# A long convolution beside a linear attention block: reciprocal by ln and exp on ACT, four more matmuls of zeros, and a new order of units

## The chip, the cores and the metric

One core of a Trainium2 chip runs the kernel. The metric is the device time of one execution in microseconds (us). The engines are named as in the profile: PE (TensorE matmul), PEld (its weight loads), DVE (VectorE), ACT (ScalarE), POOL (GpSimd), SP (SyncE, which issues all DMAs here). The engines work in parallel, each through its own queue in order; PSUM is the memory that PE writes.

## The reference

Two independent blocks over a sequence of S = 2048 rows and D = 576 columns, in bf16, whose outputs are set side by side.

```python
# A: gated long convolution
k_shift = sum over t<4 of k[s-t] * shift_k[:, t]
kv = k_shift * v
y  = causal convolution of kv with ssm_k (length 2048) along s, by FFT of length 4096
out_A = q * (y + kv * ssm_D)
# B: linear attention, 32 heads of 18
q, k, v = x @ wqkv
phi(t) = where(t > 0, t + 1, exp(t)) + 1e-6
kv = phi(k)^T v ; z = sum_s phi(k)         (per head)
o  = (phi(q) kv) / (phi(q) . z + 1e-6)
out_B = o @ wo
```

## The kernel before, in words

The program is a list of some 300 units, written out by hand as the string ORDER. A loop at the end of the kernel takes them one after the other, and each emits its instructions on the engines' queues. So the position in ORDER alone sets the order on every engine: a unit further ahead stands further ahead in each queue that it touches. What follows the slash (`k.8/3`) names the buffers: PSUM is cut into four pairs of banks, 0 to 3, and a unit that takes a pair waits until the eviction of its last user is done; some units also name a slot of a ring of SBUF buffers, ahead of the banks. The letters D, A, P choose the engine of an eviction or of an elementwise product (DVE, ACT, POOL); N leaves the unit out.

**Block A** works on five chunks of channels (four of 128, one of 64), index ci. `hl` loads ssm_k, `hd` adds ssm_D to its first element on ACT (L500), so that the skip term becomes part of the convolution. `hT` transposes h, on PE, or by a copy `hp` on ACT or POOL and a DMA transpose (L516 to L520). `kl`, `vl`, `ql` load two groups of channels of k, v, q. `cv` is the short convolution in four steps on DVE or POOL (L487 product, L489 product, L490 sum, L493 times v), with one buffer `at` for all chunks. The long convolution is a Fourier transform by matmuls in two stages, for h and for u = kv: `h1`, `u1` (matmuls L532, evicted to Ch and Cu), `ht`, `ut` (a DMA transpose to Cth, Ctu, L539), `h2`, `u2` (matmuls L555, evicted to T and SU). `pX`, `pT` are products of SU and T (L567, L569), `pS`, `pA` a difference and a sum of their halves (L572), which save matmuls of `i1` where they are made: two, three or four planes of 16 matmuls for each of its units. `i1` (L589) and `i2` (L602, L603) transform back, with an eviction to V between them; `i2` multiplies by q on DVE (L604), and `st` stores. G and F are the Fourier matrices, made by integer arithmetic on DVE and sines on ACT (`sin`, L222); F is G transposed by DMA (`FT`, L609).

**Block B** loads x in four groups (`xl`) and transposes it (`xd`, on PE L337 and L342, or by DMA). `k`, `q`, `qt` are the projections (L451, L460, L468), each followed by phi: an Exp on ACT (L443) and one DVE instruction (L444). `G` multiplies x by phi(k) (L659), `zs` sums phi(k); `wom` clears a buffer wo_M on POOL (L641), which takes the place of phi(k) and holds wo, M and the masked kv; `kv` makes the heads' kv and masks it on DVE (L687, L690, L697). `M` multiplies kv by wo (L705, L708). `den` makes the denominators of all heads in one tile of 128 x 512 (L720, L729), adds ez, which holds the epsilons (L732, L734), and takes the reciprocal into rden (L736). `bc` and `bt` spread rden over the heads' columns by matmuls (L742, L753) and multiply phi(q) by it on DVE (L746, L755). `o` and `ol` are the output products with their evictions and stores.

**At the start**, `wu` runs five matmuls of zeros on PE (L80). `Wj` spreads the weights of the short convolution over the partitions by five matmuls (W_ps, L387) that need the load of shift_k, and ACT evicts them. ACT loads its table of functions twice: one with Sin at the very start (L129), one with Exp after the last sine (L228).

Of the kernel before, what the change touches and what calls it, by code (L numbers as in the profile page):

```python
# [37 lines left out]
k.15/3 u1.0.1.0.A/2 hT.2.D/21 u1.0.0.1.A/0 u1.0.0.0.A/3 ht.1.1/0 cv.1.1.DD xd.1.T/1 k.13/2 h2.1.1.1.A/11 cv.1.2.DD
h2.1.1.0.A/0 q.3.1/3 h2.0.0.1.A/21 h2.0.0.0.A/2 ut.0.0/0 cv.1.3.DDP hl.3/0 q.3.0/0 q.1.0/1 u2.0.0.0.A/03 k.6/2
ut.0.1/1 k.7/0 u2.0.0.1.A/3 pX.0.0.D/0 qt.1/1 u2.0.1.0.A/12 u2.0.1.1.D/0 k.5/3 u1.1.1.0.A/12 kl.1 pT.0.0.D k.12/1  # L40
pX.0.1.D/1 u1.1.0.1.A/0 k.14/2 u1.1.1.1.A/3 ht.1.0/0 ql.0/1 cv.2.0.D u1.1.0.0.A/0 pT.0.1.D k.4/1 cv.2.1.DD
h1.2.1.1.A/03 pS.0.1.D pA.0.0.P ut.1.1/1 h1.2.1.0.A/2 hd.3 pA.0.1.D q.1.1/0 h2.1.0.0.A/33 h2.1.0.1.A/2 G.1/10
cv.2.2.DP ut.1.0/0 h1.2.0.0.A/3 h1.2.0.1.D/2 u2.1.1.1.A/00 zs/011 vl.1/0 u2.1.1.0.D/3 i1.0.1.1.A/12 pS.0.0.N ht.2.1/1
i1.0.0.0.D/0 cv.2.3.DDD i1.0.1.0.A/1 i1.0.0.1.A/3 u2.1.0.1.A/12 u2.1.0.0.A/0 hl.4/1 pX.1.1.D/1 ht.2.0/0 lwv FT.1.T
cv.3.0.D FT.0.T hT.3.a/20 G.3/10 pX.1.0.D/0 u1.2.1.1.A/03 pA.1.0.N cv.3.1.DD u1.2.0.0.A/2 G.0/01 u1.2.0.1.A/1
u1.2.1.0.A/3 pT.1.0.D cv.3.2.DD G.4/20 h2.2.1.1.A/00 cv.3.3.DDD h2.2.1.0.A/1 pS.1.0.N G.2/31 wom h2.2.0.0.A/22
h2.2.0.1.A/0 pA.1.1.D pT.1.1.D ut.2.0/1 hd.4 i2.0.0/1 kv/32 pS.1.1.P i2.0.1/0 h1.3.1.0.A/11 h1.3.0.1.D/3 h1.3.0.0.A/2
h1.3.1.1.A/1 u2.2.0.0.D/10 u2.2.0.1.A/2 ut.2.1/0 i1.1.1.1.A/03 cv.4.0.D i1.1.1.0.A/1 cv.4.1.DD den/0 lwo ht.3.1/1
hT.4.p/20 u2.2.1.1.A/02 i1.1.0.1.A/3 i1.1.0.0.A/1 M.2.A/2 M.3.A/3 i2.1.1/1 h2.3.1.1.A/12 cv.4.2.PP u2.2.1.0.A/0
i2.1.0/3 pX.2.0.P/1 u1.3.1.1.A/01 bc.2/20 u1.3.0.1.A/3 u1.3.0.0.A/1 bt/2 pA.2.0.N u1.3.1.0.A/3 M.1.A/0 ht.3.0/0  # L50
h2.3.1.0.D/1 h2.3.0.1.A/32 bc.0/30 h1.4.1.0.A/11 h1.4.0.1.A/2 st.0 h2.3.0.0.A/1 ut.3.0/1 pT.2.0.P bc.3/32 h1.4.1.1.A/0
M.4.A/1 M.0.A/3 bc.1/01 h1.4.0.0.A/2 pS.2.0.P u2.3.0.0.A/13 u2.3.0.1.A/2 pX.2.1.P/0 ut.3.1/0 ht.4.0/1 ql.1/1 pT.2.1.D
i1.2.0.1.A/00 i1.2.0.0.A/3 pA.2.1.D cv.4.3.DDD pS.2.1.D pX.3.0.D/1 o.1.2.AAf/12 o.0.2.AD/03 h2.4.0.1.A/21 i1.2.1.0.D/2
i1.2.1.1.A/0 pT.3.0.P u1.4.1.0.D/13 u1.4.0.0.A/1 u1.4.1.1.D/2 u1.4.0.1.A/0 h2.4.0.0.D/3 u2.3.1.1.A/01 pA.3.0.P
u2.3.1.0.A/2 ut.4.0/1 i2.2.1/0 o.1.0.AA/31 pX.3.1.D/0 pS.3.0.D pT.3.1.D o.0.0.DAf/20 i1.3.0.1.A/13 u2.4.0.1.D/11
pA.3.1.N u2.4.0.0.A/0 i2.2.0/2 pS.3.1.P i1.3.0.0.A/3 i1.3.1.1.A/1 pX.4.0.D/1 pT.4.0.D pA.4.0.D pS.4.0.D i1.3.1.0.A/0
st.1 o.1.3.DAs/23 i2.3.0/1 i1.4.0.0.A/00 i1.4.0.1.A/3 i2.3.1/2 i2.4.1/1 i2.4.0/0 st.2 o.0.3.AAs/32 o.1.1.DA/10
# [16 lines left out]
def _warm(tc, psum, K, n):  # L74

    nc = tc.nc
    zero = K.sm[:, 1984:2048].bitcast(BF)
    ps = psum.tile([128, 4, 128], FP32, name="warm_ps")
    for _ in range({'A': 5, 'B': 8, 'C': 7, 'D': 6}[n]):
        nc.tensor.matmul(ps[:], lhsT=zero, rhs=zero.unsqueeze(1).to_broadcast([128, 4, 128]), start=True, stop=True)  # L80


# [142 lines left out]
def _sine16(tc, K):  # L225
    nc = tc.nc
    nc.scalar.activation(out=K.sm[:, 1536:1984], in_=K.wi, func=ACT.Sin, scale=TWO_PI / 16, bias=K.negpi[:])
    nc.scalar.activation(out=K.warm[:], in_=K.neg1[:], func=ACT.Exp)  # L228


# [13 lines left out]
def kernel(  # L244
# [471 lines left out]
    def b_den():  # L716
        ps = psum.tile([128, 1024], FP32, name="den_ps")
        for c in range(4):
            for j in range(4):
# [14 lines left out]
        nc.vector.tensor_scalar(out=den, in0=den, scalar1=ez[:, 0:1], scalar2=None, op0=ALU.add)  # L734
        with nc.allow_low_precision(reason="the reciprocal is used as bf16"):
            nc.vector.reciprocal(out=B['rden'], in_=den)  # L736
# [152 lines left out]
```

## Time and profile before

| | |
|---|---|
| median of 3 runs | 160.94 us (159.96 to 161.66) |
| the profiled execution | span 159.3 us from its first to its last instruction; its own time is not listed |
| busy | PE 147.6, DVE 139.8, ACT 128.4, POOL 65.2 us |
| chain that ended last | PE 66%, POOL 12%, DVE 8%, DMA 6% |
| DMA | 31.92 MB in 74171 packets, 200 GB/s on average |

The busy time of PE includes the modelled ends of pipelined matmuls, so a PE at 93% is not at its peak. The chain is followed back from the last instruction, at each step to what released it. A row of the timeline gives start, busy time, engine, line, operation, output and inputs, shapes, count, and in brackets the idle time of the engine before it with what ended it. SPq is the queue of SP: its rows are the issues of DMAs. A row of windows gives the stretch, its length, the busy times of PE, PEld, DVE, ACT, POOL with their counts, the granted clock of PE, the mean busy share of the DMA engines and GB/s.

### The profile page before, as it was taken

What the parts mean: (1) busy time and instruction counts of PE and PEld (TensorE: products, weight loads), DVE (VectorE), ACT (ScalarE), POOL (GpSimd) and SP (SyncE); (2) the same over time, 40 slices, a digit from 0 to 9 for tenths busy, and PEclk for the clock granted to TensorE, in tenths of its full rate; (3) what the DMA queues carried; (4) which work ended last, traced back from release to release, by engine and by line L of the source; (5) the groups of instructions that cost most, each with busy time, mean ns of one, the idle gap of its engine ahead of it and who ended that gap; (6) DMA issues with size and microseconds to landing.
All of it is one profiled execution on the core that took longest, in us unless ns stands there. A gap on an engine that the chain in (4) does not pass through costs nothing.

```text
span 159.3 us, 4563 instructions
## 1 busy us (share of the span) xinstructions
PE 147.6 (93%) x1966; PEld 92.2 (58%) x1982; DVE 139.8 (88%) x170; ACT 128.4 (81%) x157; POOL 65.2 (41%) x67
## 2 busy tenths in 40 slices
...
GB/s 105 352 368 294 255 239 305 152 231 3 164 130 228 243 228 240 189 212 312 159 196 272 242 155 212 187 141 90 268 152 184 175 324 204 124 117 136 62 264 100
DMA packets 74171, 31.92 MB, mean 200 GB/s; under 512 B 52074, under 2 KB 73509, under 8 KB 74150
## 3 DMA queue, kind: packets, MB, share of 16 engines
...
## 4 chain that ended last, share of the span: by engine, by line
PE 66%; POOL 12%; DVE 8%; DMA 6%; issue 3%; ACT 3%; SPq 0%; DVEq 0%; ACTq 0%; POOLq 0%
PE k_ps L451 12%; PE q_ps L460 11%; PE g_ps L659 6%; PE o_ps L776 6%; PE s_ps L532 6%; POOL X L567 5%; PE s_ps L555 5%; DMA Cth<-Ch 4%; PE i_ps L589 3%; POOL T L569 3%; PE hT_ps L511 2%; DMA pqT<-in_A_shift_k_dram 2%; PE xT_ps L337 2%; PE i_ps L602 2%; PE qt_ps L468 2%
## 5 line engine op out<-in xcount | busy, mean ns | idle before, releaser
L451 PE MATMUL k_ps<-wqk,xT 128*128 128x512 bf16 (+1 forms) x154 | 21.3, 282 | 0.3
L532 PEld LDWEIGHTS <-G 128*128 128x128 bf16 x320 | 17.4, 98 | 3.7 <-issue 3.4
L299 ACT ACTIVATE Cu<-s_ps 128x1024 bf16<-128x1024 f32 (+1 forms) x18 | 16.9, 978 | 2.1 <-DMA Cth<-Ch 1.4
L460 PE MATMUL q_ps<-xT,wqk 128*128 128x512 bf16 x78 | 18.2, 379 | 0.1
L451 PEld LDWEIGHTS <-xT 128*128 128x128 bf16 x160 | 11.4, 98 | 10.5 <-issue 0.5
L299 ACT ACTIVATE Ch<-s_ps 128x1024 bf16<-128x1024 f32 (+1 forms) x17 | 15.0, 928 | 3.0 <-PE s_ps L532 2.7
L299 ACT ACTIVATE ob<-o_ps 128x576 bf16<-128x576 f32 (+1 forms) x12 | 7.5, 636 | 11.3 <-PE o_ps L768 5.1
L299 ACT ACTIVATE V<-i_ps 128x1024 bf16<-128x1024 f32 x16 | 15.7, 1034 | 1.0 <-PE i_ps L589 1.0
L659 PE MATMUL g_ps<-pk,x_sb 128*128 128x65 bf16 (+1 forms) x124 | 16.3, 283 | 0.2
L299 ACT ACTIVATE T<-s_ps 128x1024 bf16<-128x1024 f32 x16 | 15.7, 1027 | 0.5 <-POOL at L490 0.5
L490 DVE TENSOR_TENSOR at<-at 128x2048 bf16<-128x2048 bf16 (+1 forms) x13 | 14.9, 1143 | 0.7 <-POOL at L489 0.3
L489 DVE TENSOR_TENSOR at<-k,Wj 128x2048 bf16<-128x2048 bf16 (+1 forms) x13 | 14.8, 1136 | 0.4 <-POOL at L490 0.4
L776 PE MATMUL o_ps<-wo_M,pqT 128*128 128x64 bf16 (+1 forms) x108 | 13.8, 283 | 0.5 <-issue 0.5
L444 DVE SCALAR_TENSOR_TENSOR pk<-pk,k_ps 128x576 bf16<-128x576 bf16 x16 | 11.8, 751 | 2.7 <-ACT pk L443 2.6
L299 ACT ACTIVATE SU<-s_ps 128x1024 bf16<-128x1024 f32 x14 | 14.1, 1029 | 0.0
L659 PEld LDWEIGHTS <-x_sb 128*128 128x128 bf16 x128 | 8.4, 97 | 8.7 <-issue 1.1
L460 PEld LDWEIGHTS <-wqk 128*128 128x128 bf16 x80 | 7.5, 98 | 9.1 <-issue 1.1
L443 ACT ACTIVATE pk<-k_ps,neg 128x576 bf16<-128x576 f32 x16 | 11.6, 745 | 1.2 <-PE k_ps L451 0.9
L604 DVE TENSOR_TENSOR q<-i_ps,q 128x1024 bf16<-128x1024 f32 (+1 forms) x10 | 11.0, 1107 | 1.2 <-PE i_ps L603 1.2
L776 PEld LDWEIGHTS <-pqT 128*128 128x128 bf16 x112 | 7.4, 98 | 7.6 <-issue 0.9
L490 POOL TENSOR_TENSOR at<-at 128x2048 bf16<-128x2048 bf16 (+1 forms) x2 | 6.2, 3097 | 12.9 <-DVE at L489 12.9
L532 PE MATMUL s_ps<-v,G 128*128 128x128 bf16 (+1 forms) x160 | 10.5, 214 | 1.0 <-ACT Cu L299 0.4
...
## 6 DMA issues: line engine op xcount, KB each, us to landing
...
```

The costliest lines, as they stand in the source:

```text
L299: nc.scalar.activation(out=out, in_=in_, func=ACT.Copy)
L443: nc.scalar.activation(out=out_ap, in_=ps_ap, func=ACT.Exp, bias=K.neg1[0:n, :])
L444: nc.vector.scalar_tensor_tensor(out=out_ap, in0=out_ap, scalar=1.0, in1=ps_ap, op0=ALU.min, op1=ALU.max)
L451: nc.tensor.matmul(ps[:, n0:n1], lhsT=xT[r // 4][:, t, rr * 128:(rr + 1) * 128], rhs=wqk[:, t, D + n0:D + n1], start=(t == 0), stop=(t == 4))
L460: nc.tensor.matmul(ps[:, j, :], lhsT=wqk[:, t, 128 * c:128 * c + 128], rhs=xT[g][:, t, :], start=(t == 0), stop=(t == 4))
L489: on[0].tensor_tensor(out=t_, in0=kk[:, 3 - stage:19 - stage], in1=wb(stage), op=ALU.mult)
L490: on[1].tensor_tensor(out=a_, in0=a_, in1=t_, op=ALU.add)
L532: nc.tensor.matmul(ps[:, bi, 0:dc], lhsT=K.G[ri][:, b, :], rhs=xf(b), start=True, stop=True)
L555: nc.tensor.matmul(ps[q:q + 32, z, :], lhsT=K.W0[64 * z:64 * z + 64, x, :], rhs=Ct[64 * z:64 * z + 64, r, :, j, :], start=True, stop=True)
L604: nc.vector.tensor_tensor(out=qs, in0=ps[:, :, 0:dc], in1=qs, op=ALU.mult)
L659: nc.tensor.matmul(ps[:, n0:n1], lhsT=x_sb[:, r, f0:f0 + fn], rhs=pk[:, r, n0:n1], start=(r == 0), stop=(r == 15))
L776: nc.tensor.matmul(pss[i][:, n0:n1], lhsT=pqT[:, c, r * 128:(r + 1) * 128], rhs=B['M'][:, c, n0:n1], start=(c == 0 and not first), stop=(c ...
```

## The change

Three things. First, the denominators' reciprocal: DVE's addition and reciprocal go, and ACT does Ln(den + ez) in place and Exp of its negative. So that both functions are at hand, the table loaded after the last sine is now one that holds Ln and Exp. Second, nine matmuls of zeros at the start instead of five (`wu.1.A` 5, `wu.2.B` 4). Third, ORDER is another list throughout, with other engines for some evictions and products and other banks.

```diff
-io dl ix.0.0/0 hl.0/0 lz sin.1.0 eps ix.1.0/1 id ls ix.0.1 iw ix.1.1 xl.2 sin.0.0 wk wu.1.A/0 lw.2 dc/1 hd.0 Wj.A/230
+io hl.0/0 ls lz ix.0.0/0 dl wu.1.A/0 id wu.2.B/1 hl.1/1 ix.1.0/1 sin.1.0 ix.0.1 ix.1.1 sin.0.0 dc/2 hd.0 hd.1 wk iw
...
-    for _ in range({'A': 5, 'B': 8, 'C': 7, 'D': 6}[n]):
+    for _ in range({'A': 5, 'B': 4}[n]):
...
     nc.scalar.activation(out=K.sm[:, 1536:1984], in_=K.wi, func=ACT.Sin, scale=TWO_PI / 16, bias=K.negpi[:])
+    nc.scalar.preload_act_table_set("natural_log_exp_and_others")
     nc.scalar.activation(out=K.warm[:], in_=K.neg1[:], func=ACT.Exp)
...
         den = ps[:, 0:512]
-        nc.vector.tensor_scalar(out=den, in0=den, scalar1=ez[:, 0:1], scalar2=None, op0=ALU.add)
-        with nc.allow_low_precision(reason="the reciprocal is used as bf16"):
-            nc.vector.reciprocal(out=B['rden'], in_=den)
+        nc.scalar.activation(out=den, in_=den, func=ACT.Ln, bias=ez[:, 0:1])
+        nc.scalar.activation(out=B['rden'], in_=den, func=ACT.Exp, scale=-1.0)
```

What the new order moves is shown at three places. The first is the start of SP's queue, the loads: sm is D's row, h_sb the chunks of ssm_k, pqT receives shift_k, wqk are the projection weights. Before:

```order
L424 DMA sm<-in_A_ssm_D_dram 1x576
L438 DMA h_sb<-in_A_ssm_k_dram 128x2048
L373 DMA pqT<-in_A_shift_k_dram 1x2304
L319 DMA x_sb<-in_B_x_dram 128x4x576
L358 DMA wqk<-in_B_wqkv_dram 64x1152
L438 DMA h_sb<-in_A_ssm_k_dram 128x2048
L319 DMA x_sb<-in_B_x_dram 128x4x576
L361 DMA wqk<-in_B_wqkv_dram 128x4x576 x2
L404 DMA k<-in_A_k_dram 15x3x256
```

And in the change:

```order
L438 DMA h_sb<-in_A_ssm_k_dram 128x2048
L373 DMA pqT<-in_A_shift_k_dram 1x2304
L424 DMA sm<-in_A_ssm_D_dram 1x576
L438 DMA h_sb<-in_A_ssm_k_dram 128x2048
L319 DMA x_sb<-in_B_x_dram 128x4x576
L358 DMA wqk<-in_B_wqkv_dram 64x1152
L319 DMA x_sb<-in_B_x_dram 128x4x576
L361 DMA wqk<-in_B_wqkv_dram 128x4x576
L404 DMA k<-in_A_k_dram 15x3x256
```

Chunk 1 of h moved ahead of the first x, the shift weights ahead of D's row, and the second projection weight (that of q) behind the three loads of k.

The second place is DVE between the mask of z (zsel, end of `kv`) and the products of `bc` and `bt`. Before:

```order
L697 TENSOR_TENSOR zsel<-hsel,z_ps 128x160
L604 TENSOR_TENSOR q<-i_ps,q 128x8x128
L301 CAST Ch<-s_ps 128x2x32x16
L301 CAST SU<-s_ps 128x2x512
L487 TENSOR_TENSOR at<-k,Wj 128x16x64
L489 TENSOR_TENSOR at<-k,Wj 128x16x64
L490 TENSOR_TENSOR at<-at 128x16x64
L732 TENSOR_SCALAR ez<-den_ps 128x1
L734 TENSOR_SCALAR den_ps<-den_ps,ez 128x512
L736 RECIPROCAL wo_M<-den_ps 128x512
L604 TENSOR_TENSOR q<-i_ps,q 128x8x128 x2
L746 SCALAR_TENSOR_TENSOR pqT<-pqT,bc_ps 128x1024 x2
```

And in the change:

```order
L697 TENSOR_TENSOR zsel<-hsel,z_ps 128x160
L604 TENSOR_TENSOR q<-i_ps,q 128x8x128
L301 CAST Ch<-s_ps 128x2x32x16
L301 CAST SU<-s_ps 128x2x512
L569 TENSOR_TENSOR T<-SU,T 128x2048
L301 CAST V<-i_ps 128x8x32x4
L732 TENSOR_SCALAR ez<-den_ps 128x1
L301 CAST SU<-s_ps 128x2x512
L567 TENSOR_TENSOR X<-SU,T 128x2048
L604 TENSOR_TENSOR q<-i_ps,q 128x8x128 x2
L745 SCALAR_TENSOR_TENSOR pqT<-pqT,bc_ps 128x1024 x2
```

The three pieces of the last chunk's convolution moved to POOL; a T product, a V and an SU eviction and an X product came in their place; the addition and the reciprocal are gone from here and stand on ACT, behind two SU evictions and ahead of two V evictions.

The third place is POOL from the copy hp of chunk 4 on. Before, the memset of wo_M stands two rows ahead of the copy:

```order
L490 TENSOR_TENSOR at<-at 128x2048
L641 MEMSET wo_M 128x576
L572 TENSOR_TENSOR T<-T 128x2x512
L518 COPY hp<-h_sb 64x2048
L489 TENSOR_TENSOR at<-k,Wj 128x16x64
L490 TENSOR_TENSOR at<-at 128x16x64
L567 TENSOR_TENSOR X<-SU,T 128x2048
L569 TENSOR_TENSOR T<-SU,T 128x2048
```

And in the change:

```order
L490 TENSOR_TENSOR at<-at 128x2048
L518 COPY hp<-h_sb 64x2048
L641 MEMSET wo_M 128x576
L487 TENSOR_TENSOR at<-k,Wj 128x16x64
L572 TENSOR_TENSOR X<-X 128x2x512
L489 TENSOR_TENSOR at<-k,Wj 128x16x64
L490 TENSOR_TENSOR at<-at 128x16x64
L569 TENSOR_TENSOR T<-SU,T 128x2048
```

The copy moved ahead of the memset, the pieces of the last chunk's convolution came to POOL, and both X products of chunk 2 left it for DVE.

More of the change, by code (lines that the diff above doesn't have):

```diff
@@ L38 @@
[L38 to L57, printed above, removed]
@@ L58 @@
-ol.0.1/320
+io hl.0/0 ls lz ix.0.0/0 dl wu.1.A/0 id wu.2.B/1 hl.1/1 ix.1.0/1 sin.1.0 ix.0.1 ix.1.1 sin.0.0 dc/2 hd.0 hd.1 wk iw
+Wj.A/301 xl.2 hT.0.D/22 sin.1.1 lw.2 xd.2.DA/030 h1.0.0.1.D/01 sin.0.1 xl.0 lw.1 h1.0.0.0.A/2 hT.1.D/00 wm h1.0.1.0.A/3
+iv h1.0.1.1.A/1 xd.0.DD/120 kl.0 sw W k.9/3 k.10/1 cv.0.0.P k.8/2 es k.11/0 k.1/3 h1.1.1.0.A/11 k.2/2 h1.1.1.1.A/0
+cv.0.1.DD lw.0 q.2.1/3 vl.0/0 h1.1.0.1.A/1 q.0.1/2 k.0/0 ht.0.1/0 cv.0.2.PD h1.1.0.0.A/1 qt.0/3 cv.0.3.DDD h2.0.1.0.A/02
+h2.0.1.1.A/1 q.2.0/0 xl.3 ht.0.0/1 cv.1.0.D xd.3.AA/023 q.0.0/1 hl.3/1 u1.0.1.1.A/02 k.3/3 hl.2/2 hd.2 k.15/0
@@ new lines @@
+u1.0.1.0.A/2 FT.1.T u1.0.0.0.A/1 eps hT.2.D/03 u1.0.0.1.A/0 cv.1.1.PD k.13/2 ht.1.1/0 h2.1.1.0.A/11 h2.1.1.1.A/3
+cv.1.2.DD hc q.3.1/0 h2.0.0.1.A/22 h2.0.0.0.A/1 xd.1.T/1 ut.0.0/0 xl.1 cv.1.3.DDD ut.0.1/1 q.3.0/3 u2.0.0.0.A/02
+u2.0.0.1.A/0 q.1.0/1 kl.1 ht.1.0/0 k.7/2 k.6/0 u1.1.1.0.A/03 qt.1/1 u2.0.1.0.D/12 u2.0.1.1.A/0 k.5/3 u1.1.1.1.A/1
+pX.0.0.P/0 hd.3 pX.0.1.D/1 pT.0.0.D pA.0.0.P k.14/0 u1.1.0.1.A/2 k.12/3 u1.1.0.0.A/1 pA.0.1.D pT.0.1.D ql.0/1 k.4/2
+h1.2.1.1.A/10 h1.2.1.0.A/1 cv.2.0.D cv.2.1.DD q.1.1/3 h2.1.0.0.A/30 pS.0.1.D h2.1.0.1.A/2 G.1/1 cv.2.2.DP h1.2.0.1.D/0
@@ new lines @@
+ut.1.1/1 h1.2.0.0.A/2 u2.1.1.1.A/03 hl.4/2 zs/01 ut.1.0/0 u2.1.1.0.D/2 i1.0.1.1.A/00 pS.0.0.N i1.0.0.0.D/3 vl.1/0
+i1.0.1.0.A/1 cv.2.3.DDD i1.0.0.1.A/2 u2.1.0.1.A/10 hd.4 u2.1.0.0.A/3 pX.1.0.D/1 ht.2.1/1 ht.2.0/0 lwv pX.1.1.D/0
+hT.3.a/01 G.3/1 cv.3.0.D cv.3.1.DD u1.2.0.0.A/12 u1.2.1.1.A/0 G.0/3 u1.2.1.0.A/1 FT.0.T cv.3.2.DD u1.2.0.1.A/2 G.4/0
+h2.2.1.0.A/03 h2.2.1.1.A/1 cv.3.3.DDD pA.1.0.D G.2/2 ut.2.0/1 hT.4.p/02 h2.2.0.0.A/20 pT.1.1.D pS.1.1.N h2.2.0.1.A/3
+i2.0.0/1 wom kv/20 i2.0.1/3 h1.3.1.0.A/01 h1.3.0.1.D/2 h1.3.0.0.A/0 cv.4.0.P u2.2.0.0.D/03 pT.1.0.D pS.1.0.N
```

14 lines of the change are left out of this document (10 added, 4 removed).

## The prediction

> **What bounds the kernel now.** I read the page's busy shares first, then the chain that ended last, then the stages by windows, and last the queues of single engines in order of time. A span of 159.3 us belongs to the profiled execution; its own time is not listed beside it, and the median of the three timed runs, 160.94 us, lies 1.64 us above that span. I take this rest (start and end around the span) as unchanged and subtract span changes from 160.94. The three runs spread from 159.96 to 161.66, so a measurement of this kernel tells about 1% (1.6 us) from no change.
>
> ```profile
> PE 147.6 (93%) x1966; PEld 92.2 (58%) x1982; DVE 139.8 (88%) x170; ACT 128.4 (81%) x157; POOL 65.2 (41%) x67
> 0.00:14.80 14.80, 11.98 (x119) 8.98 (x120) 12.04 (x27) 12.74 (x18) 6.93 (x31) 1.00 0.89 279
> 14.80:95.30 80.50, 79.36 (x899) 45.62 (x909) 74.98 (x82) 70.47 (x83) 25.45 (x26) 1.00 1.06 209
> 95.30:122.85 27.55, 25.02 (x481) 17.52 (x479) 26.53 (x34) 24.39 (x32) 24.50 (x8) 1.00 0.89 177
> 122.85:155.30 32.45, 30.99 (x482) 20.05 (x480) 26.23 (x30) 20.43 (x27) 8.28 (x3) 1.00 0.73 176
> ```
>
> The window rows give length, then busy PE, PEld, DVE, ACT, POOL, then clock, DMA share, GB/s. Four stages differ. Up to 14.8 us (the head) PE is busy 11.98 and runs short pieces between waits. From 14.8 to 95.3 PE is busy 79.36 of 80.50: it sets the pace, so whatever the head gains is kept to 95.3 if nobody runs dry. From 95.3 to 122.85 DVE is busy 26.53 of 27.55, more than any other: here DVE's queue sets the pace, and this is where the reciprocal stands. From 122.85 the output products bring PE back (30.99 of 32.45).
>
> **The head.** These are pieces of the chain in order of time, then rows of the timeline.
>
> ```profile
> 7.23 1.71 PE hT_ps L511 x16
> 8.94 1.52 PE xT_ps L337 x16
> 12.81 1.08 PE hT_ps L511 x16
> 13.88 0.89 PE xT_ps L337 x16
> 15.27 6.00 PE k_ps L451 x48
> 1.06 2.31 PE L80 MATMUL warm_ps<-sm 128*128 128x512 bf16 x5 [1.06 <-DVE negpi L127]
> 5.15 2.08 PE L387 MATMUL W_ps<-pqT,sm 97*128 97x512 bf16 x5 [1.56 <-DMA pqT<-in_A_shift_k_dram]
> 6.20 2.22 ACT L299 ACTIVATE Wj<-W_ps 128x1024 bf16<-128x1024 f32 x3 [0.18 <-PE W_ps L387]
> 9.33 1.16 ACT L222 ACTIVATE G<-mp,negpi 128x1024 bf16<-128x1024 int32 x1
> 11.65 2.86 ACT L299 ACTIVATE Ch<-s_ps 128x1024 bf16<-128x1024 f32 x3 [0.98 <-PE s_ps L532]
> ```
>
> The same sixteen transposes take 1.71 us at 7.23 and 1.08 at 12.81, and 1.52 against 0.89 for x: early in the run PE goes at half speed, although the window's granted clock reads 1.00. The first five zero matmuls end near 3.4, PE then waits 1.56 us for the shift weights, and full speed comes inside the x transposes, near 10.0, some 4.9 us after PE began to work without a pause at 5.15.
>
> Four more zero matmuls cost 4 x 2.31/5 = 1.85 us on PE. They lie in the wait for the shift weights (1.56), and the rest, 0.3, is about what those weights gain by leaving SP ahead of D's load, so I cost them at nothing; with that cover gone they would cost up to 1.85. Now PE works from 1.06 on, so 4.9 us later is 5.9. From there W's remaining 1.3 us halve (-0.65), hT and xT save 0.63 each: -1.9 on PE alone.
>
> [...]
>
> Not all of it reaches the k products. In the new order ACT applies D to chunk 1 (0.3 us) ahead of Wj and must await that load; I put Wj near 6.5 to 8.7. Then come one sine (1.16), an x eviction 512 wide (0.5 to 0.6, its row stands below), one more sine (1.16), overlapping a little: the first Ch eviction starts near 11.5, against 11.65. But the first k unit writes bank pair 3, which was freed by the third Ch eviction (11.65 + 2.86 = 14.51), and now by the second, near 13.4. k begins near 13.6 instead of 14.8 (the row at 15.27 holds what follows its first product). **Term A: -1.2**, bounds 0 (ACT or the loads hold it as before) and -1.9.
>
> **From 14.8 to 95.3.** PE's units change places by at most a few; their sum is the same to 0.5 us. DVE, counted row by row with the durations of before, has 2.7 us less ahead of the kv masks; this alone earns nothing where PE rules. One visible stall is touched:
>
> ```profile
> 84.97 1.94 ACT L299 ACTIVATE Cu<-s_ps 128x1024 bf16<-128x1024 f32 x2 [1.43 <-DMA Cth<-Ch]
> 80.00:88.00 8.00, 7.44 (x90) 5.07 (x91) 7.97 (x10) 6.57 (x6) 0.00 (x0) 1.00 1.12 247
> ```
>
> Evictions of u1.2 wait 1.43 us for the transposes of Ch to leave their buffer. The load of h chunk 4, which stood between these two transposes on SP, is now ahead of both, but the DMA engines are full there (share 1.12). PE is busy 7.44 of 8 in that window. **Term B: -0.3**, bounds 0 and -0.6.
>
> **The DVE stage.** Rows of DVE in order of time:
>
> ```profile
> 96.80 0.97 DVE L687 TENSOR_TENSOR wo_M<-kv_ps,maskbd 126x126 bf16<-126x126 f32 x5
> 100.47 1.20 DVE L301 CAST SU<-s_ps 128x1024 bf16<-128x1024 f32 x1
> 101.60 0.86 DVE L487 TENSOR_TENSOR at<-k,Wj 128x1024 bf16<-128x1024 bf16 x1
> 102.38 0.68 DVE L489 TENSOR_TENSOR at<-k,Wj 128x1024 bf16<-128x1024 bf16 x1
> 103.09 0.69 DVE L490 TENSOR_TENSOR at<-at 128x1024 bf16<-128x1024 bf16 x1
> 103.96 0.76 DVE L734 TENSOR_SCALAR den_ps<-den_ps,ez 128x512 f32<-128x512 f32 x1
> 104.76 3.36 DVE L736 RECIPROCAL wo_M<-den_ps 128x512 bf16<-128x512 f32 x1
> 109.61 1.23 DVE L604 TENSOR_TENSOR q<-i_ps,q 128x1024 bf16<-128x1024 f32 x1 [0.42 <-PE i_ps L603]
> 122.68 1.23 DVE L569 TENSOR_TENSOR T<-SU,T 128x2048 bf16<-128x2048 bf16 x1 [0.38 <-POOL X L567]
> 124.42 0.69 DVE L489 TENSOR_TENSOR at<-k,Wj 128x1024 bf16<-128x1024 bf16 x1
> 125.14 0.69 DVE L490 TENSOR_TENSOR at<-at 128x1024 bf16<-128x1024 bf16 x1
> 127.08 1.22 DVE L567 TENSOR_TENSOR X<-SU,T 128x2048 bf16<-128x2048 bf16 x1
> 128.22 0.75 DVE L301 CAST ob<-o_ps 128x576 bf16<-128x576 f32 x1
> 128.88 1.22 DVE L301 CAST V<-i_ps 128x1024 bf16<-128x1024 f32 x1
> ```
>
> From the masks at 96.80 to the V eviction at 128.88 DVE idles 0.42 and 0.38 in all. Out of this stretch go the addition 0.76, the reciprocal 3.36 and five convolution pieces (0.86 + 0.68 + 0.69 + 0.69 + 0.69 = 3.61): -7.73. Into it come a T product 1.23, a V eviction 1.22, an SU eviction 1.20, two X products taken from POOL 2 x 1.22, one M eviction (0.75, by ob's equal width): +6.84. Net -0.89. The 0.38 that DVE waited for POOL's X goes too, since DVE makes that X itself: -1.27. The M eviction is counted; an extra wait for M's matmuls would cost its own 0.3 or so, and the 0.42 before q may vanish. **Term C: -1.3**, bounds -0.7 and -1.9.
>
> Ln and Exp on ACT have no row. The nearest are a 128x512 Exp with a pointer bias from PSUM and a 128x512 eviction from PSUM:
>
> ```profile
> L443 ACT ACTIVATE pq<-qt_ps,neg 128x512 bf16<-128x512 f32 x2 | 1.4, 690 | 0.0
> L299 ACT ACTIVATE Ch<-s_ps 128x512 bf16<-128x512 f32 x4 | 2.3, 597 | 0.5 <-PE s_ps L532 0.2
> L228 ACT ACT_TABLE_LOAD x1 | 1.3, 1283 | 0.0
> ```
>
> So 0.69 + 0.60 = 1.29 us. Below: nothing less than two 0.60 evictions, 1.2. Above: a table load on either side, 1.29 + 2 x 1.28 = 3.85. I take 1.29, since the new order has two table loads on ACT as before. Behind Ln on ACT queue two V evictions, M, T and four Cu; i2 of chunk 1 waits for V, u1.3's banks for Cu. But between the Ch evictions of h1.3 and the first ob, ACT gives up one SU, one V and one M (1.0 + 1.0 + 0.66), so it ends 1.4 us lighter, and it keeps up with term C. The reciprocal is ready some 4 us earlier than 108.1; DVE then still has an SU, an X and two q ahead of the first bc product, so nothing waits for Ln's result, only Ln for ez.
>
> **After 122.85** PE rules. One half of chunk 3 is now added before i1.3.1, which needs 16 fewer matmuls:
>
> ```profile
> 139.53 1.89 PE i_ps L589 x64
> ```
>
> 16 x 1.89/64 = 0.47. **Term D: -0.5**, bounds 0 (if PE waits for that sum) and -0.5. The end, from the last matmul at 155.3 to 159.3, keeps its eviction and store.
>
> Sum: -1.2 - 0.3 - 1.3 - 0.5 = -3.3, so a span near 156.0 and 157.7 us. The bounds add to -0.7 and -4.9: 160.2 and 156.0.
>
> **Rivals.** (1) The head earns nothing: the loads or ACT start k at 14.8 as before. For it: DMA share is full from 8 us on, and Wj on ACT is a little later. Against: k's bank pair is freed one eviction sooner. Without A the sum is -2.1: 158.8.
>
> [...] I hold this at 0.1, inside the forecast's share.
>
> (2) Slower: POOL's queue. hp of chunk 4 now stands ahead of the memset of wo_M.
>
> ```profile
> 84.10 4.64 SPq L609 DMA_TRANSPOSE F<-G  x2
> 88.84 2.46 SPq L520 DMA_TRANSPOSE hT<-hp  x1
> 93.82 0.58 POOL L641 MEMSET wo_M<- 128x576 int32 x1 [17.39 <-PE g_ps L659]
> 97.96 3.94 POOL L518 COPY hp<-h_sb 64x2048 bf16<-64x2048 bf16 x1
> hT<-hp SPq DMA_TRANSPOSE x2, 5.1
> ```
>
> This copy writes the buffer that chunk 3's hT transpose reads, so it starts when that has landed (at L), and the memset ends at L + 3.94 + 0.58. The kv masks on DVE write what the memset clears, and are due at 96.8 - 1.2 - 0.3 = 95.3, so L decides from 90.8 on, one microsecond for each. Before, the transpose was issued at 88.84 and landed some 5.1 later (the issues' median), 93.9. Now it stands on SP where the F transposes stood, 84.10, which gives 89.2. With L at 96 the masks come 5.2 us late: 157.7 + 5.2 = 162.9, slower. Full DMA engines speak for it (1.12), the earlier place on SP against it.
>
> (3) A part of that: L stays at 94 as before, the masks come 3.2 us late and the gain is eaten: 160.9, no change. POOL's longer queue (some 4 us more by its order) speaks for it, and the same earlier place against it.
>
> (4) The change does not do what it says: Ln forces a table load and the next Exp another. That is 2.57 on ACT, whose idle time in this stage is 27.55 - 24.39 = 3.2 and whose queue got lighter: within the forecast.
>
> **How the numbers follow.** Forecast with its bounds 0.55, rival 1 0.18, rival 3 0.12, rival 2 0.15 (4 lies inside). Faster by over 1% (below 159.3): the forecast and most of rival 1, 0.55 + 0.17 = 0.72. Within 1%: rival 3 and the rest, 0.13. Slower: 0.15. The likeliest alone gives 156.0 to 159.3; to leave out no more than 2 in 10 the range goes from 155.8 to 161.2.
>
> **What would show it.** Right: hT_ps near 1.1 us for the first sixteen; first k_ps near 13.6; no RECIPROCAL, two ACTIVATEs of 0.6 to 0.7; DVE busy near 136 (139.8 less 3.7 over its whole order); the masks (L687) near 95.3 and the DVE V eviction near 126; the first o_ps near 120. Wrong: hT_ps still at 1.7 (term A); the wo_M memset after 95 with DVE waiting for it (rival 2); a third table load; DVE idling over 1 us between masks and V, which would move the bound to ACT or PE.

## The result, and the profile after

The changed kernel takes 173.82 us (median of 4 runs, 173.19 to 174.27) where the kernel before takes 160.66 (159.96 to 161.66): a ratio of 1.080, interval 1.074 to 1.085. It is 13 us slower, and the forecast of 157.7 is wrong in sign. The profiled span grew from 159.3 to 172.0. Every ratio below is to runs of the kernel before taken in the same round (their medians lie between 160.99 and 161.94), by fast executions alone. From the page after: the span, the busy times, and the clock that was granted in 40 slices.

```profile
span 172.0 us, 4537 instructions
PE 151.1 (88%) x1954; PEld 94.4 (55%) x1970; DVE 145.6 (85%) x167; ACT 128.7 (75%) x158; POOL 72.5 (42%) x70
PEclk9987999999879999999999999699999999999999
```

PE has no more to do than before, apart from its slow stretches; DVE lost a reciprocal and is still busy 5.8 us longer; and the clock row has three dents, which the row before did not have. Windows over the dents (length, then busy PE, PEld, DVE, ACT, POOL, then clock, DMA share, GB/s):

```profile
8.00:16.00 8.00, 5.60 (x71) 5.60 (x72) 4.58 (x5) 4.50 (x7) 3.06 (x9) 0.79 1.13 282
40.00:48.00 8.00, 4.25 (x42) 3.12 (x42) 7.77 (x5) 4.45 (x7) 7.47 (x16) 0.87 0.66 85
104.00:112.00 8.00, 5.60 (x71) 5.23 (x71) 8.00 (x17) 3.72 (x5) 7.22 (x3) 0.79 0.81 173
```

In all three PE is idle for 2.4 to 3.8 us of 8, and the clock falls with it. In the second and third DVE and POOL are nearly full. What each kernel's profile shows at six milestones (start of the first instruction of each kind on PE, us) and at the end, with two of the experiments:

| | first k | first g | kv | den | first bc | first o | span |
|---|---|---|---|---|---|---|---|
| before | 14.84 | 66.76 | 95.15 | 101.79 | 109.95 | 122.85 | 159.3 |
| after | 16.95 | 73.97 | 106.20 | 115.08 | 123.51 | 136.56 | 172.0 |
| e_three | 13.56 | 66.76 | 96.59 | 103.98 | 112.41 | 125.45 | 160.8 |
| f_three_recip | 13.36 | 66.51 | 96.74 | 104.13 | 116.23 | 129.16 | 164.5 |

The loss after is 2.1 us at the first k, 7.2 at the first g, 11.1 at kv, 13.3 at den, 13.7 at the first o and 12.7 at the end. So it has three places, and the stretch behind the first o gives 1.0 back.

**The first, 2.1 us: the head.** The timeline of PE, first a row of the kernel before, then the kernel after:

```profile
7.02 1.91 PE L511 MATMUL hT_ps<-ident,h_sb 128*128 128x128 bf16 x16
6.17 1.16 PE L511 MATMUL hT_ps<-ident,h_sb 128*128 128x128 bf16 x16
10.40 1.07 PE L337 MATMUL xT_ps<-ident,x_sb 128*128 128x128 bf16 x16 [3.08 <-DMA x_sb<-in_B_x_dram]
13.06 1.91 PE L511 MATMUL hT_ps<-ident,h_sb 128*128 128x128 bf16 x16
16.95 6.29 PE L451 MATMUL k_ps<-wqk,xT 128*128 128x512 bf16 x49
```

The zeros did what was said of them: the first sixteen transposes take 1.16 us instead of 1.91 (the 1.71 of the prediction is the same group in the view of the chain). Then PE waits 3.08 us for x, whose load the new order issues behind that of h chunk 1. The second transposes take 1.91 again, at a granted clock of 0.50 from 13.06 to 14.97: the pause cost the clock as well.

**The second, 5.1 us: POOL and DVE at 40 us.** The timelines of POOL, DVE and PE:

```profile
40.18 4.05 POOL L489 TENSOR_TENSOR at<-k,Wj 128x2048 bf16<-128x2048 bf16 x1
40.19 5.12 DVE L487 TENSOR_TENSOR at<-k,Wj 128x2048 bf16<-128x2048 bf16 x1
46.49 1.01 PE L532 MATMUL s_ps<-v,G 128*128 128x128 bf16 x8 [3.69 <-DVE pqT L444]
47.30 1.91 PE L511 MATMUL hT_ps<-ident,h_sb 128*128 128x128 bf16 x16
```

The new order gives the first product of chunk 1 to DVE and the second to POOL. POOL's queue is held by two memsets until 40.2, so the two start together. DVE's product, 1.2 us where nothing meets it, lasts 5.12 and ends 1.08 us after POOL's (40.18 + 4.05 = 44.23; 45.31): it looks as if it stood still for POOL's whole instruction and then ran. PE waits 3.69 us for a DVE instruction queued behind it, and is then granted a clock of 0.50 (47.30 to 49.20), at which sixteen transposes take 1.91 us.

**The third, 6.1 us by den: POOL and DVE at 97 us.**

```profile
97.37 4.98 POOL L518 COPY hp<-h_sb 64x2048 bf16<-64x2048 bf16 x1 [13.78 <-PE g_ps L664]
98.63 4.81 DVE L490 TENSOR_TENSOR at<-at 128x2048 bf16<-128x2048 bf16 x1
105.29 3.08 DVE L569 TENSOR_TENSOR T<-SU,T 128x2048 bf16<-128x2048 bf16 x1
105.41 0.74 ACT L650 ACTIVATE wv_GT<-g_ps,ex 128x576 bf16<-128x576 f32 x1 [5.34 <-DVE ex L649]
106.20 1.61 PE L684 MATMUL kv_ps<-wv_GT 128*128 128x126 bf16 x25 [2.83 <-ACT wv_GT L650]
```

Again a DVE product of two SBUF tensors (4.81) ends 1.1 us after a POOL instruction (102.35; 103.44). The small copy ex (L649) stands behind it, ACT's last eviction of GT waits for ex, PE waits 2.83 us for that, and the clock falls a third time (0.64 over the next 4 us). L569 meets two more POOL instructions. The table's row of e_three will show how much of the 6.1 us goes with the copy. Four DVE rows hold all of DVE's growth: 5.12, 4.81, 3.08 and one of 1.47, against 1.22 each, are 9.6 us too long, and 145.6 - 9.6 = 136.0, which is the busy time that the forecast named.

**The DVE stage** earned nothing. ACT, PE and DVE around Ln and Exp, then DVE's first and last instruction of the stage:

```profile
117.07 0.66 ACT L734 ACTIVATE den_ps<-den_ps,ez 128x512 f32<-128x512 f32 x1 [0.20 <-DVE ez L732]
117.76 0.60 ACT L735 ACTIVATE wo_M<-den_ps 128x512 bf16<-128x512 f32 x1
118.25 1.94 ACT L299 ACTIVATE V<-i_ps 128x1024 bf16<-128x1024 f32 x2
120.24 0.22 PE L602 MATMUL i_ps<-V,F 128*128 128x128 bf16 x1 [1.79 <-ACT V L299]
121.33 2.35 DVE L604 TENSOR_TENSOR q<-i_ps,q 128x1024 bf16<-128x1024 f32 x2 [1.89 <-PE i_ps L603]
109.42 0.98 DVE L687 TENSOR_TENSOR wo_M<-kv_ps,maskbd 126x126 bf16<-126x126 f32 x5
142.29 1.22 DVE L301 CAST V<-i_ps 128x1024 bf16<-128x1024 f32 x1
```

Ln and Exp last what was estimated (0.66 + 0.60). The two V evictions queue behind them on ACT, PE waits 1.79 us for V, and DVE, now free of the reciprocal, waits 1.89 for PE. From the masks to the V eviction it is 32.9 us, against 32.1 before.

### The profile page after: what moved, and what is told of

The parts are those of the page before. It is cut to its first block, busy times and chain, and to the rows that moved or that the text cites. A ratio compares the mean times of both kernels' runs of the same rounds, so it can differ in the third digit from the quotient of the medians.

```text
span 172.0 us, 4537 instructions
## 1 busy us (share of the span) xinstructions
PE 151.1 (88%) x1954; PEld 94.4 (55%) x1970; DVE 145.6 (85%) x167; ACT 128.7 (75%) x158; POOL 72.5 (42%) x70
## 3 DMA queue, kind: packets, MB, share of 16 engines
HBM read 14.97 MB, written 4.72 MB: 114 GB/s over the span
## 4 chain that ended last, share of the span: by engine, by line
PE 44%; DVE 27%; ACT 12%; DMA 8%; issue 3%; POOL 2%; SPq 1%; DVEq 0%; ACTq 0%
PE o_ps L775 6%; PE q_ps L460 5%; PE k_ps L451 5%; DVE at L490 5%; PE s_ps L532 5%; DMA x_sb<-in_B_x_dram 5%; PE g_ps L659 4%; DVE pqT L745 4%; PE s_ps L555 4%; PE i_ps L589 4%; DMA Cth<-Ch 4%; ACT Cu L299 3%; DVE T L569 3%; DVE at L487 3%; POOL at L489 2%
## 5 line engine op out<-in xcount | busy, mean ns | idle before, releaser
L532 PEld LDWEIGHTS <-G 128*128 128x128 bf16 x320 | 19.2, 103 | 8.3 <-issue 6.6
L451 PE MATMUL k_ps<-wqk,xT 128*128 128x64 bf16 (+1 forms) x154 | 20.9, 282 | 0.3
L490 DVE TENSOR_TENSOR at<-at 128x2048 bf16<-128x2048 bf16 x11 | 17.1, 1550 | 0.5
L451 PEld LDWEIGHTS <-xT 128*128 128x128 bf16 x160 | 11.1, 98 | 10.3 <-issue 0.4
L299 ACT ACTIVATE T<-s_ps 128x1024 bf16<-128x1024 f32 x17 | 16.7, 1020 | 0.0
L489 POOL TENSOR_TENSOR at<-k,Wj 128x1024 bf16<-128x1024 bf16 (+1 forms) x5 | 14.5, 2900 | 5.0 <-DVE at L490 5.0
L490 POOL TENSOR_TENSOR at<-at 128x1024 bf16<-128x1024 bf16 (+1 forms) x4 | 10.4, 2607 | 13.8 <-DVE at L489 13.5
L299 ACT ACTIVATE V<-i_ps 128x1024 bf16<-128x1024 f32 x15 | 14.7, 1026 | 1.7 <-PE i_ps L589 1.6
L532 PE MATMUL s_ps<-v,G 128*128 128x128 bf16 (+1 forms) x160 | 11.5, 219 | 5.1 <-DVE pqT L444 3.7
L444 DVE SCALAR_TENSOR_TENSOR pk<-pk,k_ps 128x576 bf16<-128x576 bf16 x16 | 11.5, 749 | 3.1 <-ACT pk L443 3.0
L299 ACT ACTIVATE SU<-s_ps 128x1024 bf16<-128x1024 f32 x13 | 13.0, 1027 | 1.2 <-PE s_ps L555 1.2
L569 POOL TENSOR_TENSOR T<-SU,T 128x2048 bf16<-128x2048 bf16 x2 | 8.1, 4067 | 12.4 <-DVE X L567 12.4
L489 DVE TENSOR_TENSOR at<-k,Wj 128x2048 bf16<-128x2048 bf16 x10 | 12.2, 1218 | 0.4 <-POOL at L490 0.4
```

The costliest lines, as they stand in the source:

```text
L299: nc.scalar.activation(out=out, in_=in_, func=ACT.Copy)
L444: nc.vector.scalar_tensor_tensor(out=out_ap, in0=out_ap, scalar=1.0, in1=ps_ap, op0=ALU.min, op1=ALU.max)
L451: nc.tensor.matmul(ps[:, n0:n1], lhsT=xT[r // 4][:, t, rr * 128:(rr + 1) * 128], rhs=wqk[:, t, D + n0:D + n1], start=(t == 0), stop=(t == 4))
L489: on[0].tensor_tensor(out=t_, in0=kk[:, 3 - stage:19 - stage], in1=wb(stage), op=ALU.mult)
L490: on[1].tensor_tensor(out=a_, in0=a_, in1=t_, op=ALU.add)
L532: nc.tensor.matmul(ps[:, bi, 0:dc], lhsT=K.G[ri][:, b, :], rhs=xf(b), start=True, stop=True)
```

## The experiments

**a_loads** puts the load of x (and of the small projection weight) ahead again, and applies D to chunk 1 later, after the second sine. Theory P, here and below, is that a DVE product of two SBUF tensors waits until a POOL instruction that it meets has ended, as the one of 5.12 us seems to have done (it ended at 45.31, POOL's at 44.23); by it this run keeps DVE rows of 3 to 5 us and takes 170 to 172 us.

```
-io hl.0/0 ls lz ix.0.0/0 dl wu.1.A/0 ... dc/2 hd.0 hd.1 wk iw
-Wj.A/301 xl.2 hT.0.D/22 sin.1.1 lw.2 xd.2.DA/030 ...
+io hl.0/0 ls lz ix.0.0/0 dl xl.2 lw.2 wu.1.A/0 ... dc/2 hd.0 wk iw
+Wj.A/301 hT.0.D/22 sin.1.1 hd.1 xd.2.DA/030 ...
```

> The change with the load of x group 2 (and the small projection weight) issued ahead of chunk 1 of h, as before the change, and D applied to chunk 1 after the second sine. Theory S (supply): everything that went wrong starts in the head, where x landed at 10.4 and PE stood still for 3.1 us; with the load back in its place k starts at 14 or sooner, the later long rows of DVE disappear with the lateness, and the time falls to 160 to 162 us. [...]

Measured 171.1 us, ratio 1.058 (1.048 to 1.067), span 169.1. The first k starts at 13.83:

```profile
13.83 6.29 PE L451 MATMUL k_ps<-wqk,xT 128*128 128x512 bf16 x50
37.26 5.12 DVE L487 TENSOR_TENSOR at<-k,Wj 128x2048 bf16<-128x2048 bf16 x1
```

The wait of 3.08 us for x is down to 0.42, 2.9 us of span have gone with it, and the forecast's start of 13.6 is nearly there. The long DVE product stands where it stood: the load order is one of several causes, and the time is the one that theory P had.

**b_cv11** gives the second product of chunk 1 back to DVE: `cv.1.1.PD` becomes `cv.1.1.DD`.

> The change with one product of the short convolution (chunk 1, step 1, L489) on DVE instead of POOL. Theory P: the DVE product at 40.2 us, which took 5.12 us beside it, takes 1.2; PE's stall of 3.9 us at 42.6 and the cold transposes behind it (1.91 instead of 1.08 us) go; DVE gets 1.2 us more: 168.5 to 170.5 us. Theory S: DVE is late for other reasons, and 1.2 us more on it makes u no sooner: 173 to 175 us.

Measured 168.76 us, ratio 1.046 (1.037 to 1.055), span 167.2.

```profile
40.19 1.22 DVE L487 TENSOR_TENSOR at<-k,Wj 128x2048 bf16<-128x2048 bf16 x1
```

The same instruction, at the same time, now takes 1.22 us. 4.8 us of span are back, PE's wait of 3.69 us among them, though DVE got a product more to do (L489, 1.22 us).

**c_before_ln** is the kernel before with Ln and Exp alone, and with the function table that holds both.

```
-        nc.vector.tensor_scalar(out=den, in0=den, scalar1=ez[:, 0:1], ... op0=ALU.add)
-            nc.vector.reciprocal(out=B['rden'], in_=den)
+        nc.scalar.activation(out=den, in_=den, func=ACT.Ln, bias=ez[:, 0:1])
+        nc.scalar.activation(out=B['rden'], in_=den, func=ACT.Exp, scale=-1.0)
```

> Before, with nothing changed but the reciprocal (Ln and Exp on ACT, the table with both). Theory F (the forecast's term C): DVE's 4.1 us shorten the stage in which DVE sets the pace, by 1 to 3 us: 158 to 159.7 us. Theory Q (ACT's queue): Ln and Exp stand ahead of an SU and two V evictions, i2 of chunk 1 waits for these, and DVE, whose q product stands ahead of the bc products, idles as long as it saved: 160 to 162 us, with an idle of 3 us or more on DVE before q.

Measured 161.54 us, ratio 0.999 (0.994 to 1.004).

```profile
108.86 1.22 DVE L605 TENSOR_TENSOR q<-i_ps,q 128x1024 bf16<-128x1024 f32 x1 [5.28 <-PE i_ps L604]
105.78 1.95 ACT L300 ACTIVATE V<-i_ps 128x1024 bf16<-128x1024 f32 x2
```

DVE has 4.1 us less to do and idles 5.28 in the same place: its q product needs PE's i_ps, which needs V from ACT. In the order before, DVE was full there, and PE's longest wait for it in that stage is 0.32 us.

**d_before_zeros** is the kernel before with the four zeros more, as a second unit `wu.2.B/1` behind `wu.1.A/0`.

> Before, with nothing changed but four more matmuls of zeros. Forecast's mechanism: PE works without a pause from 1.1 us on, full speed comes near 6, the first transposes of h take 1.1 instead of 1.7 us, and those of x 0.9 instead of 1.5; k starts up to 1.2 us sooner: 159.5 to 160.5 us. Rival: k's bank pair is freed by ACT's third eviction at 14.5 in any case, and nothing comes through: 160.5 to 161 us.

Measured 160.35 us, ratio 0.993 (0.989 to 0.997).

```profile
6.32 1.17 PE L511 MATMUL hT_ps<-ident,h_sb 128*128 128x128 bf16 x16
13.61 6.31 PE L451 MATMUL k_ps<-wqk,xT 128*128 128x512 bf16 x50
```

k starts at 13.61, 1.23 us earlier: the size of the forecast's first term, but in the old order, where no bank pair is freed an eviction sooner, so the equal digits are chance. In the profiled execution, the slowest of the ten, the lead lasts to the first g (65.41) and then goes while ACT waits 2.33 us for the transposes of Ch, where 1.43 stood; the median keeps 0.7%.

**m_port** is a kernel by itself. In ten sections POOL runs one instruction (or none) beside three equal DVE instructions with which it shares no data. In short:

```
nc.gpsimd.tensor_tensor(out=po, in0=poa, in1=pob, op=ALU.mult)     # tt; or a copy, or a memset
for _ in range(3):
    nc.vector.tensor_tensor(out=do, in0=dva, in1=dvb, op=ALU.mult)  # ss; or one operand in PSUM, or a copy
```

Theory P expected 3 to 5 us for the first of the three beside a POOL product or copy, and the lone 1.2 beside a memset or with an operand in PSUM; on the copy from SBUF to SBUF it was silent.

> A kernel of its own that computes nothing of the reference: in ten sections one POOL instruction of about 4 us (or none) runs beside three DVE instructions that share no data with it. [...] Theory D (in the changed kernel the long DVE instruction waited for data or a buffer that the profile does not name): all of them keep their lone durations. Theory B (the two share the bandwidth): several DVE instructions are each some 1.3 to 2 times longer, and POOL's is longer by as much.

DVE's three instructions in one row each: two SBUF operands alone, beside a POOL product, beside a POOL copy, beside a POOL memset; one PSUM operand beside a POOL product; a copy from PSUM beside one; a copy from SBUF alone and beside one. Last, POOL's product and copy.

```profile
17.09 3.75 DVE L38 TENSOR_TENSOR d0ss<-dva,dvb 128x2048 bf16<-128x2048 bf16 x3
22.45 6.54 DVE L38 TENSOR_TENSOR d1ss<-dva,dvb 128x2048 bf16<-128x2048 bf16 x3
30.62 4.29 DVE L38 TENSOR_TENSOR d2ss<-dva,dvb 128x2048 bf16<-128x2048 bf16 x3
36.52 3.74 DVE L38 TENSOR_TENSOR d3ss<-dva,dvb 128x2048 bf16<-128x2048 bf16 x3
47.24 3.74 DVE L39 TENSOR_TENSOR d5ps<-acc_ps,dvb 128x1024 bf16<-128x1024 f32 x3
57.95 3.74 DVE L40 CAST d7pc<-acc_ps 128x1024 bf16<-128x1024 f32 x3
63.31 2.15 DVE L41 COPY d8sc<-dva 128x2048 bf16<-128x2048 bf16 x3
67.08 4.88 DVE L41 COPY d9sc<-dva 128x2048 bf16<-128x2048 bf16 x3
21.35 4.05 POOL L44 TENSOR_TENSOR p1tt<-poa,pob 128x2048 bf16<-128x2048 bf16 x1
29.41 1.89 POOL L45 COPY p2cp<-poa 64x2048 bf16<-64x2048 bf16 x1
```

Beside POOL's product the three take 6.54 instead of 3.75 us, 2.79 more: POOL ended at 25.40, and DVE had been ready since 22.45, 2.95 earlier. POOL's own 4.05 did not grow (4.07 in the kernel before), so the two did not slow each other down: DVE stands still. Beside a copy that ended at 31.30 it lost 0.55 of a possible 0.68. (That copy lasts 1.89 us, not the 3.94 of the copy of hp in the kernel before, so the 3 to 5 us expected beside a copy could not come.) A memset, an operand in PSUM, a copy from PSUM: nothing lost against the 3.74 or 3.75 that each takes alone. The copy from SBUF, 0.7 us each alone, lost 2.73: it stands still too. That settles theory P against D (waiting for data) and B (shared bandwidth) for these instructions.

**e_three** joins a_loads and b_cv11 and takes the copy at 97 us from POOL: `hT.4.p/02` becomes `hT.4.D/23`, PE's transposes and a DVE eviction.

> The changed kernel with three repairs together: the second group of x loaded first and the late h load moved back (a_loads), the product of chunk 1 on DVE (b_cv11), and chunk 4 of h transposed on PE and evicted by DVE instead of copied by POOL, so that the copy of 4.98 us beside DVE's L490 of 4.81 is gone. Theory P (load order and the DVE-POOL collisions are most of the 12.7 us lost): 172.0 less 2.9, less 4.8, less about 3 (the PE stall of 2.8 before kv and part of the cold clock behind it) gives a span of 161, time 160 to 164. Theory S (the new order is slower as such, and the collisions sit beside it): 166 or more.

Measured 162.17 us, ratio 1.007 (1.003 to 1.010), span 160.8. The clock row of its page, and DVE where the third place was:

```profile
PEclk9999999999999999999999999999999999999999
90.27 1.23 DVE L490 TENSOR_TENSOR at<-at 128x2048 bf16<-128x2048 bf16 x1
95.21 2.06 DVE L569 TENSOR_TENSOR T<-SU,T 128x2048 bf16<-128x2048 bf16 x1
103.13 1.49 DVE L569 TENSOR_TENSOR T<-SU,T 128x2048 bf16<-128x2048 bf16 x1
```

All three dents are gone, with 7.3 of the 8.0% lost. L490 takes 1.23 us where 4.81 stood, and PE no longer waits ahead of kv; two meetings of DVE and POOL are left there, 2.06 us where 3.08 stood and 1.49 where 1.47 did. By ratios and a 160.66 us base the load order is worth 3.6 us alone, the first collision 5.4, each to some 1.5 us by the intervals, and the rest of e_three, the second collision and its clock, 2.7; by spans they are 2.9, 4.8 and 3.5. The rest is a remainder: moving the copy was not tried alone, and the move has a price of its own, for PE's transposes of chunk 4 take 1.18 us (at 93.38). Theory P stands; 1.1 us are left.

**f_three_recip** is e_three with the reciprocal back on DVE.

> e_three with the denominators' add and reciprocal back on DVE as in the kernel before. Theory Q (Ln and Exp only move the work: DVE's 4.1 us are there waiting for PE anyway, and ACT's 1.3 us delay the V evictions): within 1.2 us of e_three either way. Theory F (the forecast's third term: DVE bounds that stage): 1.3 us or more slower than e_three, for the new order puts two DVE evictions right behind the reciprocal.

Measured 166.32 us, ratio 1.032 (1.023 to 1.040), some 4 us slower than e_three: theory Q fails here, though it held in the old order (c_before_ln).

```profile
106.92 3.36 DVE L735 RECIPROCAL wo_M<-den_ps 128x512 bf16<-128x512 f32 x1
111.41 0.23 PE L601 MATMUL i_ps<-V,F 128*128 128x128 bf16 x1 [3.92 <-DVE SU L300]
```

The new order puts an SU eviction on DVE right behind the reciprocal (at 110.19), and PE waits 3.92 us for it. From den to the first bc the table gives 12.10 us here, 8.43 in e_three and after, 8.16 before. So the order and Ln belong together: Ln pays for an order that leans on DVE there, and the pair ends where the old order with the reciprocal was.

**h_before_pd** makes the collision in the kernel before: `cv.1.0.P` and `cv.1.1.DD` become `cv.1.0.D` and `cv.1.1.PD`.

> The kernel before, with one swap: the first product of chunk 1 (cv.1.0) goes from POOL to DVE and the second (cv.1.1) from DVE to POOL, the same two instructions with the engines exchanged, as in the changed kernel. Theory P: POOL's product runs at 38 to 42 us and DVE's product of two SBUF tensors at about 40 meets it; DVE's is 2.5 to 5 us long where it was 1.2, and what is behind it (pk, the copy of hT) comes 1 to 3 us later; time 161 to 164. Theory D: DVE's product stays at 1.2 us and the time at 160 to 161.5.

Measured 163.28 us, ratio 1.012 (1.008 to 1.017).

```profile
37.19 4.06 POOL L489 TENSOR_TENSOR at<-k,Wj 128x2048 bf16<-128x2048 bf16 x1
39.51 2.83 DVE L487 TENSOR_TENSOR at<-k,Wj 128x2048 bf16<-128x2048 bf16 x1
```

POOL ends at 41.25, DVE's product 1.09 us later. Exchanging the engines of two equal products costs 1.2%.

**g_ln_v2 and h_ln_v1** look for a version that beats both: the kernel before with zeros, Ln and Exp, and the V evictions behind them on DVE, both (`i1.1.0.1.D/3 i1.1.0.0.D/1`) or the first.

> The kernel before with the four zeros more (as d_before_zeros), Ln and Exp, and the two V evictions behind them (i1.1.0.1 and i1.1.0.0) given from ACT to DVE, which in c_before_ln stood idle for 5.3 us there. Theory F2 (the third term had its gain, and it went into ACT's queue): 1 to 2 us better than the zeros alone, ratio to before 0.980 to 0.987. Theory Q2 (in the order before, PE had no wait behind the reciprocal, so nothing is to be had there): as the zeros alone, ratio 0.990 to 0.997. Theory W (DVE's evictions of 1.2 us for ACT's 1.0, in front of its products, cost something): 0.997 or more.

> As g_ln_v2, but only the first of the two V evictions goes to DVE, so that both engines evict one at the same time. Theory F2: ratio 0.980 to 0.987, the better one of the two. Theory Q2: 0.990 to 0.997. Theory W: 0.997 or more.

Measured 159.81 us, ratio 0.990 (0.988 to 0.993), and 160.97, ratio 0.997 (0.993 to 1.000). The first beats both kernels, by 1%, but isn't told from d_before_zeros (0.993, 0.989 to 0.997): theory Q2. The second lies where Q2 and W meet, and isn't the better of the two, as F2 had it. Freed from both the reciprocal and the queue behind Ln, the stage from den to the first bc still takes 8.41 us, against 8.16 before.

**j_den and k_den_cv4** ask where e_three's last 1.1 us are. j_den moves `den` behind the two V evictions on ACT; k_den_cv4 also gives chunk 4's first product to DVE (`cv.4.0.P` becomes `cv.4.0.D`).

> e_three with the denominators (den) placed behind the two V evictions on ACT instead of ahead of them, so that Ln and Exp no longer stand between two evictions that PE waits for; two PSUM places are renumbered for it (i2.1.0 and M.3). Theory Q3 (Ln and Exp cost the new order what stands behind them in ACT's queue): PE's gap of 1.79 us before the i_ps matmuls closes to under 0.7, and what is left of e_three's loss of 1.1 us (ratio 1.0068) goes: ratio 0.995 to 1.002. Theory R3 (the gap is only moved, for DVE's bc products now wait for the reciprocal): 1.003 to 1.010.

> As j_den, and the first product of chunk 4 (cv.4.0, POOL, 2.13 us) on DVE, so that DVE's L569 of 2.06 us meets only one POOL product. Theory P: L569 falls to between 1.2 and 1.5 us, DVE gets 0.7 us more for the product and 0.6 to 0.9 less there; within 0.4% of j_den. Theory V (POOL's later products, started earlier, meet other DVE instructions of two SBUF tensors): a DVE instruction over 1.6 us elsewhere, 0.4 to 1.2% slower than j_den.

j_den: ratio 1.008 (1.004 to 1.012), no better than e_three.

```profile
110.23 0.16 DVE L732 TENSOR_SCALAR ez<-den_ps 128x1 f32<-128x1 f32 x1 [0.97 <-PE den_ps L729]
114.05 2.35 DVE L745 SCALAR_TENSOR_TENSOR pqT<-pqT,bc_ps 128x1024 bf16<-128x1024 bf16 x2 [0.48 <-PE bc_ps L741]
```

PE's gap of 1.79 us is gone, as Q3 wanted, but ez now waits 0.97 us for the den matmuls, and the first bc products 0.48 where they waited 0.26: from DVE's L569 of 2.06 us to those products it takes 17.6 us in both kernels. The wait was moved, theory R3. k_den_cv4 is worse, 1.018 (1.013 to 1.024), as theory V had it:

```profile
103.48 2.12 POOL L490 TENSOR_TENSOR at<-at 128x1024 bf16<-128x1024 bf16 x1 [3.56 <-DVE at L487]
104.40 2.29 DVE L569 TENSOR_TENSOR T<-SU,T 128x2048 bf16<-128x2048 bf16 x1
```

The next POOL product came to stand beside another DVE product, 2.29 us where e_three had 1.49; and the first L569, for which theory P had 1.2 to 1.5, kept 2.04, for POOL's X now stood beside it. So e_three's remainder stays open. Its table row says where to look: the lead of 1.3 us at the first k is gone at the first g, and 1.4 more are lost by kv, the stretch in which e_three's own repair puts its 1.18 us of transposes on PE and PE then waits 0.44 for their eviction. How much of the remainder that is was not tried.

## Why the prediction was wrong, by its own steps

- **"What bounds the kernel now", the head and 14.8 to 95.3.** The working said "whatever the head gains is kept to 95.3 if nobody runs dry": somebody did. The step took every DVE and POOL instruction at its lone duration, and asked of the moves only whether sums changed (PE's are "the same to 0.5 us"). Which DVE instruction stands beside which POOL instruction wasn't looked at. That is the step that failed: the meetings stood in the sum at nothing, and the runs gave 5.4 us for the pair at 40 and, as a remainder, some 2.7 for the one at 97. The trace of before had the hint, in rows of POOL and DVE:

```profile
132.41 2.13 POOL L572 TENSOR_TENSOR X<-X 128x1024 bf16<-128x1024 bf16 x1
133.93 1.68 DVE L567 TENSOR_TENSOR X<-SU,T 128x2048 bf16<-128x2048 bf16 x1
```

  POOL ends at 134.54, DVE's X 1.07 us later, after 1.68 us for its usual 1.22. The 0.86 for an L487 of 0.68 at 101.60, which the prediction shows, is the same, at the end of the copy of hp. These are the only two such meetings in that kernel: the other fourteen of its sixteen POOL instructions over 1.9 us run beside DVE instructions with an operand in PSUM. Its order avoids the collision; the new one doesn't.
- **Term A, -1.2, was +2.1.** What the zeros do, and how much, was right: in after the five W products take 1.15 us for 2.08 and the sixteen transposes behind them 1.16 for 1.91, and in e_three, with x's load back in its place, the first Ch eviction starts at 11.38 (forecast 11.5) and k at 13.56 (forecast 13.6), while the third Ch eviction still runs, to 14.22. The condition wasn't: the working named "the loads" as a bound of 0, as if they could only withhold the gain. The row of x's load was never priced against its new place. It came late enough to add 3.08 us of waiting and to bring PE's granted clock down to 0.66 over the next 4 us. Rival 1 was the right kind, too small. The 0.1 held inside the forecast's share was for a full speed later than 5.9, which no run shows: in after, a_loads, b_cv11 and d_before_zeros the first sixteen transposes, started between 5.89 and 6.54, take 1.15 to 1.17 us.
- **Term B, -0.3,** was not tried by itself. The same wait for Cth after is 1.55 us, against 1.43, so it earned nothing.
- **Term C, -1.3, was 0.8 the other way.** The sums were right: DVE's busy time less its standing still is the 136 forecast. The reading was wrong: 26.53 of 27.55 us busy was taken for the bound. c_before_ln shows that 4.1 us can leave that queue without moving the end, and f_three_recip that in the new order they are worth some 4 us. What waits for DVE's next instruction decides, not how full DVE is. The sentence "nothing waits for Ln's result" was true, and what waits behind Ln on ACT (V, then PE) was named and then waved through because ACT's sum was lighter. The forecast had listed "DVE idling over 1 us between masks and V" as the sign of this: it idled 1.89.
- **Term D, -0.5,** came true. From the first o to the start of the last matmul it is 32.43 us before (122.85 to 155.28), 31.98 after (136.56 to 168.54) and 31.99 in e_three: 0.45 less, for the 0.47 of the working. From there to the end it is 4.02 before and 3.46 after; other runs of the old order have 3.50 to 4.47, so nothing is read from that.
- **Rivals 2 and 3** had the right instruction, the copy of hp, and the wrong harm. It started at 97.37, which less the 7.2 us lost by then is 90.2, in time for the masks by that rival's own rule. It did its damage on the way, to DVE's L490. What released it isn't settled: its row names PE's g_ps, while the transpose of rival 2 was issued at 91.11, which with that page's 5.7 us to landing gives 96.8.
- **The sum** of the likeliest values, 160.94 - 3.3, is 157.64, where 157.7 was written; nothing hangs on it.
